# Attention with masked buckets: q and k turned by the host, softmax sums multiplied in at the end of a head pair

## The chip, the cores and the metric

The kernel runs on one core of a Trainium2 chip (trn2). The metric is device time in microseconds (us), from one launch. Of the core's engines the text uses TensorE (PE for matmuls, PEld for its weight loads), VectorE (DVE), ScalarE (ACT), GpSimd (POOL) and SyncE (SP, which here only issues DMAs).

## The reference

```
mask   = q_bucket[:, :, :, None] == k_bucket[:, :, None, :]   # bucket: signs of q @ proj, k @ proj (6 bits)
scores = where(mask, q @ k.T / sqrt(D), -1e9)
attn   = exp(scores - max);  attn /= sum(attn) + 1e-9
x      = (attn @ v) laid out as [B*S, H*D]                    # B 2, H 8, S 768, D 64
x      = moe(x):   4 experts, every token through all, weights p;  512 -> 1024 -> 512
out    = moe2(x):  8 experts, the best 2 of noisy logits per token; 512 -> 1024 -> 512
```

Only the attention and the seam to the first mixture of experts (MoE) are touched by the change.

## The kernel before, in words

**Attention.** There are 16 units (batch and head, `NU`), each of 6 tiles (`NI`) of 128 queries against 768 keys, so 96 tiles (`NG`). Values in float32 are kept as two parts, a high one in the PE's fp32r form and the rest, so that products are nearly exact.

For every unit the kernel loads q, k and v (`load`, L295) with tokens on the partitions, splits them (`split_q`, `split_k`, `split_q_rest`, `split_v`, all on POOL through the helpers at L273 and L276), and turns them on PE, since the scores need head dimensions on the partitions: `turn_half` makes three transposes of 128x128 for each half of k (L323) and three matmuls against the identity for each half of q's high part and of q's rest (L325), and ACT copies each half out of PSUM (L326). That is 18 PE instructions and 6 ACT copies a unit. Copies between the partition halves follow: `copy_q` and `lend_k` by DMA on SP (L283), `copy_k` on POOL (L285). `project_bits` (L356, 357) gives the hash bits, `mask_q` and `mask_k` (L360, L364) write them, scaled to 2^30, into the lower 64 rows of q2 and k2, so that the score matmul itself adds the mask.

For every tile: `scores` (four matmuls, L378, into a PSUM tile `big`), `clamp` (DVE, L385, takes the mask out and the row minimum), `exps` (ACT, L392, with the row sum into `rec`), `norm` (DVE adds 1e-9 at L398 and inverts at L400; POOL multiplies the whole 128x768 tile, L273), `turn` (six transposes on PE, L413; high part by ACT, L416; rest by DVE, L417), and for every three tiles `apply` (12 matmuls, L429 and L430, into `pa`). `gather` (ACT, L443) and `add_up` (DVE, L450) add the two halves of `pa` for a head into `xp`, and for every two heads `split` (POOL, L273; DVE, L458) writes the parts xth and xtl that the MoE reads.

**Order.** The attention is written out by hand in `tc.manual_schedule()`: every `block(order, lag, every, count, f)` puts calls of f into a list at a slot, counted in tiles, and a place within it; the sorted list is the order of the instructions on each engine. Nothing is bound to a time: an engine goes on as soon as its next instruction has its inputs.

**First MoE.** It follows as groups `n` of (batch, expert, quarter) with a hand-made order of their own; `first_layer` is L639 to L641, the second layer L657 to L659. Group 0 uses PSUM tiles `big`, group 1 needs the PSUM tiles that attention gives back. `stage_first` (L215) and `stage_part` (L169) load weights by SP into four buffers. Near the end of attention SP also issues `fill_scratch` (L155 to L163: zeros into the padding and the output, start values into the routing table) and ACT issues `small_inputs` (L136 to L139). The start of the kernel holds ten warming matmuls (L465), `projections` (L107), and the splitting of the first two w1 groups on DVE (`early_weights`, L178, L180).

Of the kernel before, what the change touches and what calls it, by code (L numbers as in the profile page):

```python
# [30 lines left out]
QB = 1  # L31
# [5 lines left out]
def lsh_attention_moe_kernel(ctx, tc, q, k, v, proj, probs, w1, w2, w_gate, w_noise, noise, w1b, w2b, out):  # L37
    nc = tc.nc
    B, H, S, D = q.shape
# [4 lines left out]
    NB = proj.shape[1]  # L44
# [26 lines left out]
    identr = const.tile([P, P], F32R, name="identr")  # L71
    nc.vector.tensor_copy(identr, ident)
# [27 lines left out]
    nc.vector.tensor_reduce(lessq[32:64], ident[32:64, 32:32 + NB], axis=AX.X, op=ALU.add, negate=True)  # L100
    lessk = const.tile([P, 1], F32, name="lessk")
    nc.vector.memset(lessk, 0.0)
    nc.vector.tensor_reduce(lessk[64:96], ident[64:96, 64:64 + NB], axis=AX.X, op=ALU.add, negate=True)


    def projections(pool):
        praw = pool.tile([P, NB], F32, name="praw", bufs=1)  # L107
        for r in range(2):
            nc.sync.dma_start(praw[r * D:(r + 1) * D], proj)
        ph = pool.tile([P, NB], F32R, name="ph", bufs=1)  # L110
        nc.vector.tensor_copy(ph, praw)
        pl = pool.tile([P, NB], F32R, name="pl", bufs=1)
        nc.vector.tensor_sub(pl, praw, v32(ph))
        pjq = pool.tile([P, P], F32R, name="pjq", bufs=1)
        pjk = pool.tile([P, P], F32R, name="pjk", bufs=1)
        pjl = pool.tile([P, P], F32R, name="pjl", bufs=1)
        for t in (pjq, pjk, pjl):
            nc.vector.memset(v32(t), 0.0)
        for o in (0, 32):
            nc.vector.tensor_scalar_mul(pjq[0:D, o:o + NB], v32(ph)[0:D], -1.0)  # L120
            nc.vector.tensor_scalar_mul(pjq[D:2 * D, o:o + NB], v32(pl)[D:2 * D], -1.0)
            nc.vector.tensor_copy(pjk[:, 64 + o:64 + o + NB], v32(ph))
            nc.vector.tensor_scalar_mul(pjl[0:D, o:o + NB], v32(ph)[0:D], -1.0)
            nc.vector.tensor_copy(pjl[D:2 * D, 64 + o:64 + o + NB], v32(pl)[D:2 * D])
        return pjq, pjk, pjl
# [9 lines left out]
    def small_inputs(n):  # L135
        nc.scalar.dma_start(pr.rearrange("p b i e -> p b (i e)"), probs.rearrange("(b p i) e -> p b (i e)", b=B, i=NI))  # L136
        nc.scalar.dma_start(nz.rearrange("p b i e -> p b (i e)"), noise.rearrange("(b p i) e -> p b (i e)", b=B, i=NI))
        nc.scalar.dma_start(wgn[:, :, 0:E2], w_gate.rearrange("(p c) e -> p c e", p=P))
        nc.scalar.dma_start(wgn[:, :, E2:], w_noise.rearrange("(p c) e -> p c e", p=P))  # L139
# [11 lines left out]
    yd = dram.tile([CAP, DM], F32, name="yd")  # L151
    table = dram.tile([E2 * ROWS_E, 2], I32, name="table")
    tv = table.rearrange("(e r) c -> e r c", e=E2)
    def fill_scratch(n):
        nc.sync.dma_start(x2d[0:PADS].rearrange("(t p) d -> p t d", p=P),  # L155
                          zero[:, :DM].unsqueeze(1).to_broadcast([P, PADS // P, DM]))
        nc.sync.dma_start(out.rearrange("(t p) d -> p t d", p=P),
                            zero[:, :DM].unsqueeze(1).to_broadcast([P, NT + PADS // P, DM]))
        nc.sync.dma_start(tv[1:, 0:CAP].rearrange("e (p s) c -> p e (s c)", p=SLOT_P),
                          pad_a.rearrange("p s c -> p (s c)").unsqueeze(1).to_broadcast([SLOT_P, E2 - 1, 2 * SLOT_S]))  # L160
        nc.sync.dma_start(tv[0, 0:CAP].rearrange("(h p s) c -> p h (s c)", h=2, p=SLOT_P),
                          pad_a.rearrange("p (h s) c -> p h (s c)", h=2))
        nc.sync.dma_start(tv[:, CAP:].rearrange("e (p j) c -> p e (j c)", p=P),  # L163
                            pad_b.rearrange("p j c -> p (j c)").unsqueeze(1).to_broadcast([P, E2, 2 * OVER_J]))
# [102 lines left out]
    with tc.tile_pool(name="at", bufs=2, side="right") as at, tc.tile_pool(name="psa", bufs=3, space=PSUM) as pss:  # L267
# [22 lines left out]
        def load(u):  # L290
            b, h = divmod(u, H)
            raws[u] = {}
            for nm, src, bufs in (("q", q, 2), ("k", k, 2), ("v", v, 3)):
                raws[u][nm] = ai.tile([P, NI, D], F32, tag=nm + "r", name=nm + "r", bufs=bufs)
                nc.sync.dma_start(raws[u][nm], src[b, h].rearrange("(p i) d -> p i d", i=NI))  # L295

        def split_q(u):
            qd = raws[u]["qd"] = ai.tile([P, NI, D], F32R, tag="qd", name="qd", bufs=QB)
            pool_scale(qd, raws[u]["q"], engine=nc.gpsimd)
# [28 lines left out]
        def turn_q(u, a):  # L328
            if a == 0:
                units[u] = {t: ai.tile([P, S], F32R, tag=t, name=t) for t in ("q1", "k1", "q2", "k2")}  # L330
# [981 lines left out]
```

## Time and profile before

| | |
|---|---|
| median of 3 runs | 1135.02 us (1134.3 to 1142.12) |
| the profiled execution's own time | 1136.44 us |
| its span, first to last instruction | 1134.7 us |
| PE, PEld busy | 97%, 88% of the span |
| DVE, ACT, POOL busy | 67%, 47%, 37% |
| mean granted TensorE clock | 0.987 of full speed |

A share is an average over stages. Attention fills about the first 272 us; the two MoE layers fill the rest. In rows of a timeline the first figure is the start in us from the span's start, the second the length; "[1.14 <-DMA q<-k]" says that the engine had been idle 1.14 us and what ended that. "x6" says that six neighbours are merged into a row.

### The profile page before, as it was taken

To read this page: it belongs to the slowest core of one execution; us is meant where nothing else is said; L and a number is where in the kernel's file an instruction comes from. 1 tells how busy PE (TensorE), PEld (TensorE's weight loads), DVE (VectorE), ACT (ScalarE), POOL (GpSimd) and SP (SyncE) were. 2 spreads that over 40 slices of the span, in tenths; PEclk is the share of its full clock that TensorE was granted. 3 is DMA by queue.
4 is the path that set the end of the run, shared out by engine and by line. 5 is a ranking of instruction groups with operands and counts; after the bars stand their busy time and mean duration, and the time that the engine had idled before them with its cause. 6 is when DMAs were issued, how large, how long until landed. Compare 5 with 4: busy or idle time off the path is not lost. (4 is left out here: it accounts for less than half of the span.)

```text
span 1134.7 us, 16731 instructions
## 1 busy us (share of the span) xinstructions
PE 1104.2 (97%) x6134; PEld 1003.4 (88%) x6135; DVE 756.1 (67%) x1549; ACT 529.2 (47%) x979; POOL 425.3 (37%) x464
## 2 busy tenths in 40 slices
PE   7999999998999999999999999999989999999997
PEld 5999999997888988899988988988879999999995
DVE  7999999996866565647766566535425666576651
ACT  4989999884334343333434342213214334443430
POOL 7888888861000000000000003025266626765434
PEclk8999999999999999999999999999799999999998
DMA  4222222182222122222322124114066468787864
GB/s 135 70 71 71 70 52 63 47 254 61 75 75 75 57 71 60 75 75 69 99 75 75 56 74 145 43 47 87 14 158 184 121 195 230 185 213 209 225 157 64
DMA packets 107166, 118.55 MB, mean 104 GB/s; under 512 B 13920, under 2 KB 78560, under 8 KB 106432
## 3 DMA queue, kind: packets, MB, share of 16 engines
q1 hardware_dynamic: 91948, 100.00, 30.2%
q0 software_dynamic: 9728, 15.18, 6.9%
q10 hardware_dynamic: 5404, 2.25, 0.9%
q8 instruction: 50, 0.82, 0.3%
q14 instruction: 36, 0.29, 0.1%
HBM read 90.60 MB, written 20.90 MB: 98 GB/s over the span
## 5 line engine op out<-in xcount | busy, mean ns | idle before, releaser
L178 POOL TENSOR_SCALAR w1h<-stage 128x1024 fp32r<-128x1024 f32 x4 | 5.1, 1277 | 418.5 <-PE sm L640 418.5
L1120 POOL DMA_INDIRECT xb<-x2d,at x96 | 104.1, 1085 | 35.2 <-issue 29.6
L273 POOL TENSOR_SCALAR ex<-ex,rec 128x768 f32<-128x768 f32 x96 | 92.4, 962 | 38.8 <-DVE rec L400 17.0
L417 DVE TENSOR_TENSOR el<-sm,eh 128x384 fp32r<-128x384 f32 x192 | 97.6, 548 | 12.9 <-ACT eh L416 11.4
L180 DVE TENSOR_TENSOR w2l<-stage,w2h 128x1024 fp32r<-128x1024 f32 x64 | 77.4, 1221 | 38.8 <-ACT w2h L176 36.1
L241 DVE SCALAR_TENSOR_TENSOR hl<-big,hh 128x864 fp32r<-128x864 f32 (+2 forms) x44 | 42.1, 957 | 88.6 <-ACT hh L239 68.5
L234 PE MATMUL big<-gh,w1h 128*128 128x432 f32 (+1 forms) x288 | 100.3, 348 | 0.6 <-ACT gh L945 0.6
L235 PE MATMUL big<-gl,w1h 128*128 128x432 f32 (+1 forms) x288 | 100.0, 347 | 0.1
L236 PE MATMUL big<-gh,w1l 128*128 128x432 f32 (+1 forms) x288 | 99.8, 346 | 0.0
L392 ACT ACTIVATE ex<-ms,mn 128x768 f32<-128x768 f32 x96 | 89.8, 935 | 7.9 <-DVE ms L385 3.7
L378 PE MATMUL big<-k,q 128*128 128x512 f32 (+1 forms) x384 | 90.6, 358 | 2.4 <-POOL k L364 2.4
L645 ACT ACTIVATE hh<-mx 128x384 fp32r<-128x384 f32 x72 | 37.8, 525 | 117.8 <-DVE mx L731 59.2
L385 DVE TENSOR_SCALAR_CACHE_REDUCE ms<-big 128x768 f32<-128x768 f32 x96 | 90.4, 942 | 3.2 <-PE big L378 2.9
L239 ACT ACTIVATE hh<-big 128x864 fp32r<-128x864 f32 (+2 forms) x44 | 35.7, 811 | 118.5 <-PE big L236 85.7
L659 PE MATMUL big<-w2h,hl 128*128 128x512 f32 x224 | 88.4, 395 | 0.5 <-DVE hl L646 0.5
L416 ACT CAST eh<-sm 128x384 fp32r<-128x384 f32 x192 | 82.0, 479 | 14.3 <-PE sm L413 13.3
L657 PE MATMUL big<-w2h,hh 128*128 128x512 f32 x224 | 88.2, 394 | 0.0
L658 PE MATMUL big<-w2l,hh 128*128 128x512 f32 x224 | 88.1, 393 | 0.0
L180 DVE TENSOR_TENSOR w1l<-stage,w1h 128x1024 fp32r<-128x1024 f32 x64 | 79.2, 1238 | 12.9 <-ACT w1h L176 10.6
L963 POOL DMA_INDIRECT out_dram<-xg,lts x28 | 52.9, 1889 | 76.6 <-DVE xg L961 66.8
L413 PE MATMUL sm<-ident,ex 128*128 128x128 f32 x576 | 80.5, 274 | 1.1 <-POOL ex L273 0.9
L413 PEld LDWEIGHTS sm<-ident,ex 128*128 128x128 f32 x576 | 65.9, 140 | 5.3 <-POOL ex L273 1.5
(277 smaller groups left out, 3142.1 us busy)
## 6 DMA issues: line engine op xcount, KB each, us to landing
stage<-in_moe_w_dram SPq DMA_DIRECT2D x96, 512.0 KB
stage<-in_moe_w_dram SPq DMA_DIRECT2D x58, 256.0 KB
yd<-yt SPq DMA_DIRECT2D x24, 216.0 KB
ya<-yd SPq DMA_DIRECT2D x6, 864.0 KB
out_dram<-zero SPq DMA_DIRECT2D x1, 4096.0 KB
qr<-in_q_dram SPq DMA_DIRECT2D x16, 192.0 KB
kr<-in_k_dram SPq DMA_DIRECT2D x16, 192.0 KB
vr<-in_v_dram SPq DMA_DIRECT2D x16, 192.0 KB
```

The source lines that it names most:

```text
L180: rest.tensor_sub(lo, st, v32(hi))
L234: nc.tensor.matmul(o, wh[:, d, fs], xh[:, d, cols], start=(d == 0), stop=False)
L235: nc.tensor.matmul(o, wh[:, d, fs], xl[:, d, cols], start=False, stop=False)
L236: nc.tensor.matmul(o, wl[:, d, fs], xh[:, d, cols], start=False, stop=(d == ND - 1))
L273: engine.tensor_scalar(o, i, scale, bias, op0=ALU.mult, op1=ALU.add)
L378: nc.tensor.matmul(ps[:, n0:n1], w_[:, qs], x_[:, n0:n1], start=st, stop=not st)
L385: nc.vector.tensor_scalar(ms, ps[:, :S], MASKED, 3.0e38, op0=ALU.min, op1=ALU.min, accum_out=mn)
L392: nc.scalar.activation(ex, ms, AF.Exp, bias=mn, scale=-1.0, accum_out=rec)
L413: nc.tensor.transpose(pt[:, c * P:(c + 1) * P], ex[:, cc * P:(cc + 1) * P], ident)
L417: nc.vector.tensor_sub(el[:, cs, js], ptv, v32(eh)[:, cs, js])
L659: yield lambda: nc.tensor.matmul(outs[j], hl[:, k, js], wh[:, i], start=False, stop=sp)
L1120: nc.gpsimd.indirect_dma_start(out=xb[:, b], out_offset=None, in_=x2d.rearrange("t (g x) -> (t g) x", g=4), in_offset=bass.IndirectOffsetO ...
```

## The change

The host (outside the timed launch) hands q and k over as one array `qk` with the head dimension on the rows: rows 0 to 63 hold q of a head and rows 64 to 127 its k, in 768 columns; and `proj` already laid out in a 128x128 tile.

- `load` reads one 128x768 tile z a unit; `scale_z`, `split_z`, `split_z_rest` (POOL, 128x768 each) scale and split q and k together. The first unit does it on DVE in halves (`open_z`, `open_z_rest`).
- `spread_k` (three copies) and `spread_q` (one) bring parts to the other 64 partitions, by SP's DMAs of 64x768; for the first unit on ACT and POOL. All of `turn_half` and its callers go.
- `project_bits` keeps three matmuls a half.
- `norm` goes. `exps` writes its row sums into a column of a tile `rec` of 128x32 per unit; `invert` (DVE, three instructions a unit) adds 1e-9, inverts and turns it in blocks of 32; `note` (four DMAs on SP) writes rows of it to DRAM (`norms`), `spread_norms` (one DMA) reads them back as 64 equal rows into `share`.
- `gather` has two ACT copies a half (into xa and xb), `add_up` and the new `share_out` (a multiplication with `share`) run on POOL once for two heads, 128x768 each. The last pair has its own `finish`, on POOL, DVE and ACT, in parts.
- `early_weights` becomes `early_stage` and eight `early_split` on POOL, later in the order. `small_inputs` is issued by SP. `fill_scratch` is cut into six pieces, which SP issues in MoE groups 1 to 6, behind that group's weight loads.
- All slots of the order are new; each is now one number, in tiles.

```diff
 def load(u):
-    for nm, src, bufs in (("q", q, 2), ("k", k, 2), ("v", v, 3)):
-        raws[u][nm] = ai.tile([P, NI, D], F32, tag=nm + "r", ...)
-        nc.sync.dma_start(raws[u][nm], src[b, h].rearrange("(p i) d -> p i d", i=NI))
+    z = ai.tile([P, S], F32, tag="z", name="z", bufs=2)
+    if u == 0:
+        for a, queue in enumerate((nc.sync, nc.scalar)):
+            queue.dma_start(z[:, a * QW:(a + 1) * QW], qk[b, h][:, a * QW:(a + 1) * QW])
+    else:
+        nc.sync.dma_start(z, qk[b, h])
...
+def scale_z(u):
+    pool_scale(z, z, halve)
+def split_z(u):
+    pool_scale(parts_for(u)["q1"], raws[u]["z"])
+def split_z_rest(u):
+    split_rest(units[u]["q2"], raws[u]["z"], units[u]["q1"])
+def moved(u, o, i, engine=nc.scalar):
+    if u > 0:
+        nc.sync.dma_start(v32(o), v32(i))
...
+def spread_k(u, part):
+    o, i = ((k1[0:D], q1[D:2 * D]), (k2[0:D], q1[D:2 * D]), (k1[D:2 * D], q2[D:2 * D]))[part]
+    moved(u, o, i, nc.gpsimd if part == 1 else nc.scalar)
+def spread_q(u):
+    moved(u, q1[D:2 * D], q1[0:D])
...
-def turn_half(a, src, dst, rows, scale):
...
 def exps(g):
-    nc.scalar.activation(ex, ms, AF.Exp, bias=mn, scale=-1.0, accum_out=rec)
+    nc.scalar.activation(ex, ms, AF.Exp, bias=mn, scale=-1.0, accum_out=recs[u % 2][:, i:i + 1])
-def norm(g, part):
-    if part == 0:
-        nc.vector.tensor_scalar_add(rec, rec, 1e-9)
-    else:
-        nc.vector.reciprocal(rec, rec)
-        pool_scale(ex, ex, rec)
+def invert(u):
+    nc.vector.tensor_scalar_add(rec[:, :NI], rec[:, :NI], 1e-9)
+    nc.vector.reciprocal(rec[:, :NI], rec[:, :NI])
+    nc.vector.transpose(rates[u], rec)
+def note(u):
+    for g in range(4):
+        nc.sync.dma_start(norms[u].rearrange("(i g r) -> g i r", g=4, r=32)[g], rec[32 * g:32 * g + NI])
+def spread_norms(u):
+    nc.sync.dma_start(shares[u // 2][mine], norms[u:u + 1].to_broadcast([D, S]))
...
-def gather(hf):
-    nc.scalar.copy(xp[mine, qs], pa[rest, :QW])
-def add_up(hf):
-    nc.vector.tensor_add(x, x, o)
+def gather(hf, part):
+    nc.scalar.copy(pairs[u // 2][part][mine, qs], pa[(rest, mine)[part], :QW])
+def add_up(pair):
+    nc.gpsimd.tensor_add(xa, xa, xb)
+def share_out(pair):
+    nc.gpsimd.tensor_mul(xa, xa, shares.pop(pair))
...
+block(-12.56, NI, NU, load, begin=(-43.40, -14.36,))
+block(-7.82, NI, NU, scale_z, first=1)
+block(-5.52, NI, NU, split_z, first=1)
+block(-5.03, NI, NU, split_z_rest, first=1)
+block(-5.02, NI, NU, load_v, begin=(-22.88, -12.53,))
+block(-4.74, NI, NU, spread_k, 0, begin=(-11.98,))
+block(-4.51, NI, NU, project_bits, 0, begin=(-15.79,))
+block(-2.85, NI, NU, spread_k, 2, begin=(-18.14,))
+block(-2.80, NI, NU, spread_k, 1, begin=(-14.56,))
+block(-2.52, NI, NU, project_bits, 1, begin=(-8.36,))
+block(-1.40, NI, NU, spread_q, begin=(-4.53,))
+block(-1.34, NI, NU, mask_q, begin=(-4.45,))
+block(-0.89, NI, NU, mask_k, begin=(-2.15,))
+block(-0.20, 1, NG, scores, begin=(-0.76,))
+block(6.48, NI, NU, invert)
+block(10.49, NI, NU, note)
+block(11.73, NI, NU, spread_norms)
+block(0.00, 1, 2, early_stage, begin=(14.31, 21.80,))
+block(22.45, 2 * NI, NU // 2 - 1, add_up)
+block(23.36, 2 * NI, NU // 2 - 1, share_out)
...
+            fill_scratch(n - 1)
```

## Rows read from the trace of the kernel before

**Rows 1.** Stretches: busy us of PE, PEld, DVE, ACT, POOL; granted clock; DMA share; GB/s.
```profile
16.00:22.00 6.00, 4.86 (x19) 4.38 (x20) 3.05 (x9) 2.81 (x6) 5.35 (x7) 0.50 0.33 100
...
120.00:150.00 30.00, 30.00 (x215) 27.98 (x215) 28.67 (x81) 27.64 (x65) 26.23 (x31) 1.00 0.25 67
```

**Rows 2.** Timeline of DVE: clamps of tiles 1, 7, 91 and 96.
```profile
16.16 0.94 DVE L385 TENSOR_SCALAR_CACHE_REDUCE ms<-big 128x768 f32<-128x768 f32 x1
...
29.16 0.94 DVE L385 TENSOR_SCALAR_CACHE_REDUCE ms<-big 128x768 f32<-128x768 f32 x1
...
242.66 0.96 DVE L385 TENSOR_SCALAR_CACHE_REDUCE ms<-big 128x768 f32<-128x768 f32 x1
...
252.90 0.93 DVE L385 TENSOR_SCALAR_CACHE_REDUCE ms<-big 128x768 f32<-128x768 f32 x1
```

**Rows 3.** Timeline of PE: half of q's rest, half of k, each with its successor.
```profile
107.52 0.35 PE L325 MATMUL sm<-identr,qrest 128*64 128x128 f32 x3
107.71 0.84 PE L413 MATMUL sm<-ident,ex 128*128 128x128 f32 x6
...
121.18 0.49 PE L323 MATMUL sm<-ident,kd 128*128 128x128 f32 x3
121.43 0.94 PE L378 MATMUL big<-k,q 128*128 128x512 f32 x4
```

**Rows 4.** Groups of PEld by line, 120.98 to 151.28 (two units).
```profile
L323 PEld LDWEIGHTS sm<-ident,kd 128*128 128x128 f32 x12 | 1.5, 141 | 0.1
...
L325 PEld LDWEIGHTS sm<-identr,qd 128*64 128x64 f32 x12 | 1.2, 136 | 0.2 <-DVE el L417 0.2
```

**Rows 5.** Timeline of DVE: the last small step of a tile, and an add_up.
```profile
118.05 0.15 DVE L400 RECIPROCAL rec<-rec 128x1 f32<-128x1 f32 x1
118.12 0.94 DVE L385 TENSOR_SCALAR_CACHE_REDUCE ms<-big 128x768 f32<-128x768 f32 x1
...
104.87 0.53 DVE L450 TENSOR_TENSOR xp<-xp,pa 64x384 f32<-64x384 f32 x1
```

**Rows 6.** A transposition on DVE, from the answer on tile yt.
```profile
L1143 DVE STREAM_TRANSPOSE yt<-padded x24: 698/705/715, 884.7 to 1086.1; 128x512 f32<-128x512 f32 x24
```

**Rows 7.** Groups of ACT by line: q's copies out of PSUM.
```profile
L326 ACT ACTIVATE q<-sm 64x384 fp32r<-64x384 f32 x64 | 30.5, 481 | 13.7 <-PE sm L325 11.2
```

**Rows 8.** Groups of POOL by line: the multiplication of norm, a subtraction.
```profile
L273 POOL TENSOR_SCALAR ex<-ex,rec 128x768 f32<-128x768 f32 x96 | 92.4, 962 | 38.8 <-DVE rec L400 17.0 <-PE sm L413 11.8 <-ACT ex L392 7.1
...
L276 POOL TENSOR_TENSOR qrest<-qr,qd 128x384 fp32r<-128x384 f32 x16 | 17.0, 1063 | 0.2
```

**Rows 9.** Timeline of SP: copies across partitions, one alone, one ahead of loads.
```profile
72.04 0.47 SPq L283 DMA_DIRECT2D q<-q  x1
75.93 0.47 SPq L283 DMA_DIRECT2D q<-k  x1
```

**Rows 10.** A stretch after the first of them: clock, DMA share, GB/s.
```profile
74.00:75.00 1.00, 1.00 0.05 12
```

**Rows 11.** Timeline of PE: the matmul that waits for the second of them.
```profile
80.31 0.44 PE L356 MATMUL sm<-q,pjl 128*128 128x384 f32 x1 [1.14 <-DMA q<-k]
```

**Rows 12.** Timeline of the start: POOL, then PEld.
```profile
4.80 0.51 POOL L273 TENSOR_SCALAR qd<-qr 128x384 fp32r<-128x384 f32 x1 [2.52 <-DMA qr<-in_q_dram]
...
15.21 0.30 PEld L378 LDWEIGHTS big<-k,q 128*128 128x128 f32 x2 [2.77 <-POOL k L364]
```

**Rows 13.** Timeline of the seam to the MoE: ACT, then PE.
```profile
260.36 0.94 ACT L392 ACTIVATE ex<-ms,mn 128x768 f32<-128x768 f32 x1 [3.01 <-DMA nz<-in_moe_noise_dram]
...
272.09 0.45 PE L639 MATMUL sm<-xth,w1h 128*128 128x384 f32 x1 [1.15 <-DVE xp L450]
```

**Rows 14.** Timeline of SP: the costliest piece of fill_scratch to issue.
```profile
232.80 9.40 SPq L159 DMA_DIRECT2D table<-pad_a  x1
```

**Rows 15.** Waits of SP, 330 to 460: us in total, times, longest.
```profile
SPq L215 <- DVE w2l L180: 82.6, 8, 10.5
SPq L169 <- DVE mw L621: 37.0, 9, 5.0
```

More of the change, by code (lines that the diff above doesn't have):

```diff
@@ L430, in apply @@
                 nc.tensor.matmul(pa[:, :QW], vx[:, c], el[:, c], start=False, stop=(c == NI - 1))
-        def gather(hf):
+        def gather(hf, part):
             u, half = divmod(hf, 2)
             b, h = divmod(u, H)
-            del halves[hf]
-            pa = sums.pop(hf)
-            if hf % 4 == 0:
-                pairs[u // 2] = at.tile([P, S], F32, tag="xp", name="xp")
-            xp = pairs[u // 2]
+            pa = sums[hf]
+            if hf % 4 == 0 and part == 0:
+                pairs[u // 2] = [tl.tile([P, S], F32, tag=t, name=t, bufs=XB) for t in ("xa", "xb")]
             mine = slice((h % 2) * D, (h % 2 + 1) * D)
@@ L454, in split, with finish @@
             cs = slice(b * S, (b + 1) * S)
+            xa, _ = pairs[pair]
             if part == 0:
-                pool_scale(xth[:, c, cs], pairs[pair], engine=nc.gpsimd)
+                pool_scale(xth[:, c, cs], xa, engine=nc.gpsimd)
             else:
-                nc.vector.tensor_sub(xtl[:, c, cs], pairs.pop(pair), v32(xth)[:, c, cs])
+                nc.vector.tensor_sub(xtl[:, c, cs], xa, v32(xth)[:, c, cs])
+                del pairs[pair]
+        def finish(n):
+            pair = NU // 2 - 1
+            b, c = divmod(pair, H // 2)
+            xa, xb = pairs[pair]
+            what, step = divmod(n, 3)
+            rows = slice(0, D) if what == 0 else slice(D, 2 * D)
+            cols = slice(0, S) if what == 0 else slice((what - 1) * QW, what * QW)
+            x, hi, lo = (t[rows] for t in (xa, xth[:, c, b * S:(b + 1) * S], xtl[:, c, b * S:(b + 1) * S]))
+            if step == 0:
+                engine = nc.vector if what == 2 else nc.gpsimd
+                more = sums.pop(4 * pair + 3)[rows, :QW] if what == 2 else xb[rows, cols]
+                engine.tensor_add(x[:, cols], x[:, cols], more)
+                engine.tensor_mul(x[:, cols], x[:, cols], shares[pair][rows, cols])
+            elif step == 1:
+                if what == 2:
+                    nc.scalar.copy(hi[:, cols], x[:, cols])
+                else:
+                    pool_scale(hi[:, cols], x[:, cols])
+            else:
+                nc.vector.tensor_sub(lo[:, cols], x[:, cols], v32(hi)[:, cols])
         NU = B * H
@@ L466, in lsh_attention_moe_kernel, with block, early_stage, early_split @@
             events = []
-            def block(order, lag, every, count, f, *args, begin=()):
-                for n in range(count):
-                    slot = begin[n] if n < len(begin) else (lag + n * every, order)
-                    events.append((*slot, f, n, args))
+            def block(at, every, count, f, *args, begin=(), first=0):
+                for n in range(first, count):
+                    events.append((begin[n - first] if n - first < len(begin) else at + n * every, f, n, args))
             early_w1 = []
-            def early_weights(n):
+            def early_stage(n):
                 stage_first(n)
-                plain[n] = split_plain(n, nc.vector)
+                plain[n] = [wa.tile([P, ND, 2, P], F32R, tag=t, name=t, bufs=2) for t in ("w1h", "w1l")]
+            def early_split(k):
+                n, part = divmod(k, 4)
+                ds = slice(part % 2 * (ND // 2), (part % 2 + 1) * (ND // 2))
+                hi, lo = plain[n]
+                if part < 2:
+                    pool_scale(hi[:, ds], raw1[n][:, ds])
+                else:
+                    split_rest(lo[:, ds], raw1[n][:, ds], hi[:, ds])
             def stage_weights(n):
```

261 lines of the change are left out of this document (124 added, 137 removed).

## The prediction

> **What bounds the kernel now.** I read four views in this order. First the busy shares: PE is busy for 97% of the span at a granted clock of 0.987, all other engines for two thirds or less, so time is won where PE has less to do or waits less. Second the table of stretches [rows 1]: in attention the other engines are nearly full too. Of 30 us PE has 30.00, DVE 28.67, ACT 27.64, POOL 26.23, and the reader is to see that a saving on PE alone is worth something only as far as DVE, ACT and POOL also shrink. Third the starts of the clamps, one a tile [rows 2]: tile 7 (first of unit 1) at 29.16, tile 91 (first of unit 15) at 242.66, so a unit takes (242.66 - 29.16) / 14 = 15.25 us; ahead of it lies a start of 16.16 us to the first clamp, behind it a seam from the last clamp at 252.90 to the first MoE matmul that needs attention's PSUM. Fourth single instructions in the timelines, for prices. Everything after the seam is PE-bound MoE that the change leaves as it is, except for what SP issues there.
>
> So the sum has three terms: 15 units' worth of steady work (14 periods, and the 13.0 us of unit 0, in which the turning for units 1 and 2 is done), the start, and the seam.
>
> **PE in a unit.** It loses 18 instructions. Ends of matmuls are modelled, so I price by the distance to the next start [rows 3]: half of q, three matmuls, 107.71 - 107.52 = 0.19; half of k, three transposes, 121.43 - 121.18 = 0.25. A unit has four halves of q (high part and rest) and two of k: 4 x 0.19 + 2 x 0.25 = 1.26 us. Nothing is added on PE, since the hash keeps six matmuls. PE's unit becomes 15.25 - 1.26 = 13.99 us, and 15 x 1.26 = 18.9 us is the first term.
>
> A rule of the Trainium skill (Perfetto Trace Analysis, Identifying the Most-Contended Engine) says that the matmuls' busy share is a poor measure of how full PE is, and that the weight loads' share is a good one. By this rule PE had room left in attention, since its weight loads fill 27.98 of 30 us [rows 1], and the removed ones, three groups of twelve in two units [rows 4], would count by their own length. What that would make of the time is the first rival below.
>
> **DVE in a unit.** It loses twelve small steps of norm, each 0.07 by the distance to the next start (118.12 - 118.05) and 0.15 by its length, and two add_ups of 0.53 [rows 5]: 0.84 to 1.8, and 1.06. It gains invert: two small steps of the same kind (0.07 to 0.15) and a transposition of 128x32. The only transposition in the trace has 512 columns and takes 0.70 [rows 6]; a small step's 0.07 is the lower end. So 0.2 to 1.0 is added, and the net is -0.9 to -2.7; I take -1.6, with invert near its lower end, since 32 columns are nearer to a small step than to 512. DVE's 28.67 of 30 is 14.6 a unit; it becomes 13.0, and 13.7 at worst. Both lie under PE's 13.99, so DVE hides, with 0.3 us to spare at worst; without that cover its excess would come on top of each unit.
>
> **ACT and POOL in a unit.** ACT loses six copies out of PSUM of 0.48 [rows 7] and gains two of the same shape for gather: -1.9, from 14.1 to 12.1. POOL loses six multiplications of 0.96 [rows 8] and two subtractions of 1.06 (q's and k's rests), 7.9, besides the other splits of q and k and one copy. It gains scale_z and split_z (same shape as the multiplication, 0.96 each), a rest of twice the columns (2 x 1.06), and for two units one add_up and one share_out of twice the columns, 2.12 each, so 2.12 a unit: 6.2. At most 13.3 - 1.7 = 11.6, hidden. The early w1 splits, now on POOL too, are a few us once, in the middle of units with over 2 us to spare each.
>
> **SP in a unit.** This is where the change adds waits. SP had five DMAs a unit (three loads, two copies) and gets eleven (two loads, four copies, four notes, one read back); at 0.47 to issue [rows 9] that is 5.2 of 14 us. How long a copy takes to land is bounded by two rows: the one issued alone at 72.04 has moved its data by about 74, since in the next microsecond the DMA share is 0.05 [rows 9, 10], so 2.0 us is the lower end; the one issued at 75.93 ahead of loads lets PE go at 80.31 [rows 11], 4.4 us. I take 2.0 to 4.4 for every kind of new DMA, for the write to DRAM and the read back as well, which the trace doesn't show at this size.
>
> The tight one is spread_q: it overwrites the lower half of q1, which the hash matmuls and two copies read, so it can be issued only after project_bits' second half (slot -2.52) and has to land before the unit's first scores (-0.20). That is 2.32 tiles of 13.99 / 6 us, 5.4 us, against 0.47 + 2.0 to 4.4. It fits, with 0.5 us left at the bad end. Ahead of it on SP stand note's four DMAs (4 x 0.47 = 1.9 us). Their input, invert, is four tiles older than their slot, so SP will have issued them while it waited for project_bits; I cost them at nothing. If they fall into the window after all, a unit is late by up to 1.9 + 0.47 + 4.4 - 5.4 = 1.4 us. What queues behind spread_q is spread_norms, which waits for note's landing, and then the next unit's copies, for which most of a unit is left.
>
> **The start.** Now the first full scores wait for mask_k at 15.21, after POOL began on q at 4.80 [rows 12]; the first clamp is at 16.16. After: z's halves are the first DMAs of two queues, so work can begin near 4.8 or earlier. Four opening steps on DVE at about 0.53 (2.1), three matmuls (0.5, an estimate from 0.19 for three smaller ones), two bits (1.1), mask_k on POOL (0.96), scores (0.94 [rows 3]): 4.8 + 5.6 = 10.4, and the first clamp near 10.7, since the second half of z and proj come by a queue that starts later. ACT's copies for the other halves (three of 64x768, 0.96 each by twice [rows 7]) lie beside that. The gain is 5.5; the ends are 2 and 6.5, since now the clock falls to 0.50 from 16 to 22 us after PE had little to do [rows 1], and the same may come earlier.
>
> **The seam.** From 252.90 to 272.09 it takes 19.2 us [rows 2, 13]. ACT stands 3.01 us behind the issue of small_inputs, which goes to SP, and PE 1.15 us for the last add_up. New on the path: the last unit's sums have to travel through DRAM before DVE's part of finish frees `pa`. From the last clamp: clamp and exps 1.9, invert 0.2 to 1.0, note 1.9 to issue and 2.0 to 4.4 to land, the read back 2.0 to 4.4, add and multiply 1.1: 9.1 to 14.7 us, under the 19.2 - 4.2 = 15.0 us that PE has to do there anyway. So the gain is 3.0 + 1.2 = 4.2; ends +2 (DVE stands in that wait while the MoE's splits queue behind it) and -6.
>
> **fill_scratch in the MoE.** The start values of the table take 9.40 us to issue [rows 14], the second piece no more, so up to 18.8 us in one group. SP idles 82.6 / 8 + 37.0 / 9 = 14.4 us a group [rows 15]. At worst a weight load is 4.4 us late, and it is for the group after the next: nothing.
>
> **Sum.** -18.9 - 5.5 - 4.2 = -28.6 us. Against the profiled execution's own 1136.4 that is 1107.8; the median of the runs is 1.4 lower, which gives 1106.4. The case's own range is 1100 to 1113.
>
> **Rivals.**
> 1. The weight loads are the measure of PE's time (the rule above). The removed ones are 1.5 for k, 1.2 for one part of q and, its twin taken as equal, 1.2 for the other [rows 4], 3.9 in two units, so 1.95 a unit; at the share of now, 27.98 of 30, that is 2.1 us of time a unit and 31.4 in all: 1136.4 - 31.4 - 5.5 - 4.2 - 1.4 = 1094. For it: DVE, ACT and POOL all shrink by more than 1.3. Against: DVE at 13.0 leaves 15.25 - 2.1 = 13.15 barely reachable.
> 2. spread_q lands late and PE waits before each unit: 0.6 us costs 9 (1115), 1.4 costs 21 (1127). For it: PE already waited 1.14 us for such a copy. Against: the slots leave 5.4 us.
> 3. SP becomes the bound, and the kernel is slower. If everything on SP is serial, a unit is note 1.9 + 4.4, three copies 1.4 + 4.4, spread_q 0.47 + 4.4: 17.0 us, +1.75 a unit, 26 in all, and 1135 + 26 - 9.7 = 1151. It decides from a unit of 15.25 + 9.7 / 15 = 15.9 us. Against: with 2.0 to land the same chain is 9.8 us, and the three copies don't wait for note.
>
> **How the numbers follow.** Forecast 0.62, rival 1 0.14, rival 2 0.19, rival 3 0.05. The range 1095 to 1121 takes in the forecast, most of rival 1 and the better half of rival 2. A measurement tells about 1%, 11 us. Over 1% faster is below 1123.7: the forecast, rival 1 and three quarters of rival 2, 0.90; within 1% the rest of rival 2 and a little of rival 3, 0.06; slower 0.04.
>
> **What would show it.** Right: clamps of successive units 13.5 to 14.2 us apart; first clamp at 10 to 12; from the last clamp to the first MoE matmul on `sm` 14 to 17 us; PE still without gaps in attention, ACT and DVE below 93% there; the rest from that matmul to the end as long as now, 1134.7 - 272.1 = 862.6. Wrong: PE waits for a DMA of q1 at each unit's first scores (rival 2); SP never idle and units over 15 us apart (rival 3); units at 13.2 or less (rival 1); or a MoE longer than 862.6 by over 3 us, with waits for stage loads near group 7.

## The result, and the profile after

The changed kernel takes 1106.99 us (median of 4 runs, 1105.27 to 1122.99) against 1134.66 us of the kernel before on the same chip (4 runs, 1131.45 to 1142.12). The ratio is 0.9732 with a 95% interval of 0.9671 to 0.9792: faster, by 2.7%; they leave out the run of 1122.99 us, which ran in a slower state of the chip (mean granted clock 0.980, against 0.989 in the other three). The profiled execution has an own time of 1105.56 us and a span of 1103.5 us, at a mean granted clock of 0.989. Forecast were 1106.4 us and a range of 1095 to 1121.

The marks of the stages first: the clamps of tiles 1, 3, 7, 91 and 96 on DVE in the changed kernel (start, duration, instruction, and in brackets what it idled for), which answer to [rows 2].

```profile
10.48 0.96 DVE L387 TENSOR_SCALAR_CACHE_REDUCE ms<-big 128x768 f32<-128x768 f32 x1 [1.49 <-PE big L380]
...
15.76 0.96 DVE L387 TENSOR_SCALAR_CACHE_REDUCE ms<-big 128x768 f32<-128x768 f32 x1 [0.81 <-PE big L380]
...
23.49 0.95 DVE L387 TENSOR_SCALAR_CACHE_REDUCE ms<-big 128x768 f32<-128x768 f32 x1
...
216.76 0.95 DVE L387 TENSOR_SCALAR_CACHE_REDUCE ms<-big 128x768 f32<-128x768 f32 x1
...
228.13 0.95 DVE L387 TENSOR_SCALAR_CACHE_REDUCE ms<-big 128x768 f32<-128x768 f32 x1
```

And on PE the two waits between tiles 2 and 3, and the first MoE matmul on `sm`, which answers to the last line of [rows 13].

```profile
11.76 0.69 PE L358 MATMUL sm<-q,pjh 128*128 128x384 f32 x1 [0.27 <-POOL q L273]
...
13.66 0.69 PE L358 MATMUL sm<-q,pjh 128*128 128x384 f32 x1 [0.90 <-POOL q L276]
...
243.38 0.44 PE L695 MATMUL sm<-xth,w1h 128*128 128x384 f32 x1 [1.15 <-DVE xa L496]
```

From these marks the whole difference of the spans, 31.2 us, can be laid out:

| stage | before, us | after, us | difference | forecast |
|---|---|---|---|---|
| to the first clamp | 16.16 | 10.48 | -5.68 | -5.5 |
| tiles 1 to 7 (unit 0) | 13.00 | 13.01 | 0.0 | -1.3 |
| 14 units, tiles 7 to 91 | 213.50 | 193.27 | -20.2 | -17.6 |
| tiles 91 to 96 | 10.24 | 11.37 | +1.1 | 0 |
| last clamp to first matmul on `sm` (the seam) | 19.19 | 15.25 | -3.9 | -4.2 |
| from there to the end | 862.6 | 860.1 | -2.5 | 0 |

A unit is now 193.27 / 14 = 13.805 us instead of 15.25. The 14 units in one stretch each, the kernel before and the changed one (columns as in [rows 1]):

```profile
29.16:242.66 213.50, 211.66 (x1511) 198.25 (x1509) 202.28 (x568) 195.25 (x448) 182.32 (x215) 1.00 0.28 78
```

```profile
23.49:216.76 193.27, 192.79 (x1269) 177.29 (x1266) 180.68 (x413) 174.69 (x393) 132.89 (x124) 1.00 0.46 117
```

So PE's busy time fell by (211.66 - 192.79) / 14 = 1.35 us a unit and its idle time, 1.84 and 0.48 us in all, by 0.10. The stage of tiles 1 to 7, which gained nothing, in both:

```profile
16.16:29.16 13.00, 11.73 (x64) 10.06 (x65) 9.72 (x31) 9.10 (x21) 11.11 (x15) 0.75 0.16 47
```

```profile
10.48:23.49 13.01, 11.59 (x55) 9.23 (x54) 9.91 (x22) 8.69 (x18) 7.97 (x9) 0.74 0.37 91
```

Two more stretches of the changed kernel; the second line answers to the 30 us shown there:

```profile
10.00:24.00 14.00, 12.58 (x62) 10.15 (x63) 10.42 (x22) 8.96 (x19) 8.92 (x10) 0.76 0.36 89
...
120.00:150.00 30.00, 29.93 (x198) 27.63 (x197) 28.36 (x68) 27.41 (x63) 21.05 (x19) 1.00 0.48 123
```

PE is full in the steady state as before, and per unit it is DVE 28.36 x 13.805 / 30 = 13.05 us, ACT 12.6, POOL 9.7. The waits of SP from 20 to 215 us (total, times, longest):

```profile
SPq L418 <- POOL xa L473: 24.6, 6, 4.7
SPq L326 <- PE sm L358: 22.8, 9, 3.6
```

SP stands in waits of this kind for a good part of attention, so it is not full, and in the same stretch the only wait recorded for PE is 0.2 us, once, for DVE: none is for the DMA of q1. What is new at the end of a unit, the inversion on DVE and the way of the sums through DRAM, in the last unit: DVE, then SP, then POOL.

```profile
233.34 0.16 DVE L404 TENSOR_SCALAR rec<-rec 128x6 f32<-128x6 f32 x1
233.53 0.19 DVE L405 RECIPROCAL rec<-rec 128x6 f32<-128x6 f32 x1
233.76 0.21 DVE L407 STREAM_TRANSPOSE rect<-rec 128x32 f32<-128x32 f32 x1
...
234.00 1.31 SPq L412 DMA_DIRECT2D norms<-rect  x4
236.50 0.48 SPq L418 DMA_DIRECT2D share<-norms  x1
...
239.78 1.27 POOL L497 TENSOR_TENSOR xa<-xa,share 64x384 f32<-64x384 f32 x1 [1.84 <-DMA share<-norms]
```

The inversion takes 233.89 - 233.34 = 0.55 us to the next start; from the first DMA to the first use of what comes back are 5.8 us. The first MoE matmul on `sm` does not wait for this: it is let go by DVE's addition at 242.76, which waited for ACT's copy of `pa`, and ACT for PE.

### The profile page after: what moved, and what is told of

It is laid out like the page before. It is cut to its first block, busy times and chain, and to the rows that moved or that the text cites. A ratio compares the mean times of both kernels' runs of the same rounds, so it can differ in the third digit from the quotient of the medians.

```text
span 1103.5 us, 15809 instructions
## 1 busy us (share of the span) xinstructions
PE 1081.4 (98%) x5846; PEld 977.4 (89%) x5847; DVE 728.6 (66%) x1364; ACT 508.4 (46%) x918; POOL 368.8 (33%) x364
## 3 DMA queue, kind: packets, MB, share of 16 engines
q10 hardware_dynamic: 4092, 2.41, 0.9%
## 5 line engine op out<-in xcount | busy, mean ns | idle before, releaser
L436 DVE TENSOR_TENSOR el<-sm,eh 128x384 fp32r<-128x384 f32 x192 | 102.7, 549 | 16.7 <-ACT eh L435 15.1
L435 ACT CAST eh<-sm 128x384 fp32r<-128x384 f32 x192 | 86.8, 478 | 17.6 <-PE sm L432 16.9
L432 PE MATMUL sm<-ident,ex 128*128 128x128 f32 x576 | 91.1, 275 | 1.0 <-DVE el L436 0.6
L179 DVE TENSOR_TENSOR w1l<-stage,w1h 128x1024 fp32r<-128x1024 f32 x62 | 75.7, 1221 | 14.4 <-ACT w1h L175 9.4
L432 PEld LDWEIGHTS sm<-ident,ex 128*128 128x128 f32 x576 | 70.8, 141 | 11.7 <-DVE el L436 4.9
L1195 PE MATMUL sm<-hh,w2h 128*128 128x432 f32 x192 | 68.5, 357 | 0.6 <-issue 0.6
```

Source lines behind the costliest of these rows:

```text
L179: rest.tensor_sub(lo, st, v32(hi))
L432: nc.tensor.transpose(pt[:, c * P:(c + 1) * P], ex[:, cc * P:(cc + 1) * P], ident)
L436: nc.vector.tensor_sub(el[:, cs, js], ptv, v32(eh)[:, cs, js])
```

## The experiments

My theory: in the steady state PE sets the unit and the 18 instructions that left it are the gain, provided DVE shrinks with it; start and seam come as the prediction's parts say. Rivals: DVE or POOL set the unit before; start and seam came from something else. The kernel before took 1124.94 us (median) on one of the chips used and 1150.92 us (one run) on another, so stages are compared by the marks of each kernel's own profile.

**PE's instructions back.** The changed kernel with 18 small matmuls and transposes a unit that nobody reads.

```
+def turn_again(k):   # parts 0 to 3: like half of q; 4, 5: like half of k
...
+    for i in range(HALF):
+        if part < 4: nc.tensor.matmul(t[:D, i * P:(i + 1) * P], pjs[0][:, 0:D], pjs[0], start=True, stop=True)
+        else: nc.tensor.transpose(t[:, i * P:(i + 1) * P], ident, ident)
...
+block(0.50, 0.97, NU * NI, turn_again)
```

> The changed kernel with 18 PE instructions a unit put back that nothing reads: twelve matmuls of 64 columns of weights against 128 columns and six 128x128 transposes, in six groups of three, one a tile. Nothing else differs. Theory (PE's order of instructions sets the unit): a unit takes 13.81 + 1.26 = 15.07 us, 14.9 to 15.2, and the span grows by 16 x 1.26 = 20 to about 1124. Rival (another engine sets the unit and PE's work was hidden): the unit stays under 14.3 and the span under 1111.

Measured: clamp of tile 7 at 22.20, of tile 91 at 238.21, so 15.43 us a unit; ratio 0.9955 (0.9939 to 0.9972). The stretch of this kernel, and the added lines in it:

```profile
120.00:150.00 30.00, 30.00 (x220) 28.26 (x218) 26.69 (x60) 25.23 (x58) 18.55 (x18) 1.00 0.40 106
...
L511 PE MATMUL sm<-pjh 128*64 128x128 f32 x27 | 3.1, 224 | 0.0
L513 PE MATMUL sm<-ident 128*128 128x128 f32 x12 | 2.0, 272 | 0.0
```

PE is gapless, DVE has fallen to 26.7 of 30. The theory holds; the price is 15.43 - 13.81 = 1.62 us for 18 instructions at these slots rather than 1.26. Why it is more than the distances to the next start, which I had read off one neighbour, was not taken apart.

**DVE's steps back.** PE stays relieved; DVE alone gets twelve small steps and two additions a unit on tiles of their own.

```
...
+def tiny(g):
+    nc.vector.tensor_scalar_add(dum[0][:, :1], dum[0][:, :1], 1e-9)
+    nc.vector.reciprocal(dum[0][:, :1], dum[0][:, :1])
+def more_add(hf):
+    nc.vector.tensor_add(dum[1][:D], dum[1][:D], dum[1][:D])
...
+block(1.39, 1, NG, tiny)
+block(7.70, HALF, 2 * NU, more_add)
```

> Tests whether the load that left VectorE counted. VectorE alone gets back per tile the two small steps (0.07 to 0.15 us each) and per half of a unit one 64x384 addition (0.53 us), on tiles of their own that nobody reads; TensorE, ScalarE, GpSimd and the copies stay as in the changed kernel. Theory (TensorE sets the unit and VectorE has 13.05 us of the 13.81): VectorE comes to 13.05 + 6 x 0.14 + 2 x 0.53, that is 14.9 us, or 15.9 if each of the small steps takes its full row; it takes over and the unit comes out at 14.9 to 16.0, so without the move of the additions and the reciprocals TensorE's saving would have been worth little. Rival (VectorE's room inside the unit takes it up): unit at or under 14.2.

Measured: tile 7 at 22.57, tile 91 at 237.91, so 15.38 us a unit; one run took 1120.44 us. Its 14 units in one stretch, and one pair of the small steps with its successor on DVE:

```profile
22.57:237.91 215.34, 205.73 (x1265) 174.82 (x1263) 211.49 (x609) 176.90 (x394) 139.54 (x124) 1.00 0.41 105
```

```profile
137.35 0.13 DVE L519 TENSOR_SCALAR dum<-dum 128x1 f32<-128x1 f32 x1
137.51 0.16 DVE L520 RECIPROCAL dum<-dum 128x1 f32<-128x1 f32 x1
137.59 0.54 DVE L436 TENSOR_TENSOR el<-sm,eh 128x384 fp32r<-128x384 f32 x1
```

Now DVE is the full one. A dependent pair takes 0.16 + 0.08 = 0.24 us by the starts, six pairs 1.4, two additions 0.9: 13.05 + 2.3 = 15.4, the unit. So PE's relief hangs on DVE's. The two halves are not alike, though. With PE's work back the unit is 15.43, and before it was 15.25: DVE's relief alone would have bought nothing. The other run puts back more than had left: DVE is busy 211.49 / 14 = 15.11 us a unit here and was 202.28 / 14 = 14.45 in the kernel before, because the inversion stays and the added steps stand beside it. DVE is full here at 211.49 of 215.34 us, a share of 0.982; with the load of the kernel before it would set the unit at 14.45 / 0.982 = 14.7 us (an estimate from these rows). So by this estimate PE's relief alone would have bought some 0.5 of the 1.45 us. In the kernel before, PE was the full engine (1.84 us idle in the 14 units) and DVE stood close behind it.

**The multiplication back.** Per tile again: rec added to and inverted on DVE, ex multiplied on POOL ahead of the transposes; no DMA of sums. In the second kernel the additions of the halves also go back to DVE.

```
...
+def norm(g, part):
+    if part == 0: nc.vector.tensor_scalar_add(rec, rec, 1e-9)
+    else:
+        nc.vector.reciprocal(rec, rec)
+        pool_scale(ex, ex, rec)
...
-block(6.48, NI, NU, invert)
+block(1.35, 1, NG, norm, 0)
+block(1.45, 1, NG, norm, 1)
...
-block(2.78, 1, NG, turn, 0)
+block(3.78, 1, NG, turn, 0)
```

> The changed kernel with norm as before: DVE's two small steps and POOL's multiplication for every tile, turn and all behind it one tile later, no invert, note, spread_norms, share_out. PE has the changed kernel's work. Theory (PE sets the unit, DVE lies just under it at 13.1): DVE gains twelve small steps of 0.07 to 0.15 and loses invert (about 0.5), so 13.4 to 14.4, and the unit takes 13.8 to 14.4 us; span 1103 to 1112. Rival (taking norm out of the tiles is what paid): unit above 14.6, span above 1114.

> As the one before, and add_up on DVE as before too (one ACT copy a half, DVE adds out of PSUM; the last pair splits like the others). So only the turning of q and k is left of the change in attention. Theory (the unit goes to the fullest of PE and DVE): DVE 14.4 to 15.2 a unit, so it takes over from PE: unit 14.4 to 15.1 us, span 1113 to 1123, which gives back a third to all of the 1.45 us a unit. Rival (PE alone counts): unit 13.8 to 14.0 and span at most 1106.

Measured: 20.35 and 19.75 us a unit, spans 1187.5 and 1183.4 us; the second has a ratio of 1.0517 (1.0495 to 1.0538). Both are misses. The waits of PE in the first of them, 40 to 220 us, and its stretch:

```profile
PE big L380 <- POOL k L366: 22.0, 9, 3.7
PE sm L358 <- POOL q L276: 11.3, 9, 1.3
```

```profile
120.00:150.00 30.00, 20.04 (x125) 17.02 (x123) 20.89 (x60) 18.66 (x41) 21.83 (x22) 1.00 0.18 47
```

No engine is full. POOL has 21.83 x 20.35 / 30 = 14.8 us of work a unit, which I had left out of the sum, and works in order: each multiplication waits for its tile's inverted sum, and behind it stand the split of the next unit's z and the masks, for which PE waits. The slots are mine, so the 20 us are a price of this order, not of the multiplication. What the runs show is that in this order the multiplication and the splits of q and k do not go together in POOL's queue; what taking the multiplication out is worth by itself stays open.

**Where the seam came from, first try.** The copies of the small inputs back on ACT.

```
-def small_inputs(n):  nc.sync.dma_start(...)
+def small_inputs(n):  nc.scalar.dma_start(...)
```

> The changed kernel with the four small loads before the MoE issued by ACT again, at the same slot. The prediction's account of the seam (ACT stood 3.0 us behind them, and PE with it): from the last clamp to the first MoE matmul on sm 15.25 + 3.0 = 18 us, span about 1106.5. Rival (the seam is full of PE work that has to be done anyway, and ACT's stand is covered): 15.2 to 16 us, span 1103 to 1104.

Measured: last clamp 226.40, first matmul on `sm` 241.65: 15.25 us, to the hundredth that of the changed kernel, although ACT stands behind the issues again, 2.41 us for the 3.01 of [rows 13]:

```profile
229.59 0.48 ACT L435 CAST eh<-sm 128x384 fp32r<-128x384 f32 x1 [2.41 <-DMA stage<-in_moe_w_dram]
```

In the changed order this stand costs nothing. For the kernel before the run doesn't settle it, because there the last tile's exps, which came at 260.36 behind that stand, were followed by norm: DVE's reciprocal at 263.98, then POOL's multiplication (its row names PE's transposes, which ended last before it), for which PE waited.

```profile
264.32 1.44 POOL L273 TENSOR_SCALAR ex<-ex,rec 128x768 f32<-128x768 f32 x1 [5.79 <-PE sm L413]
...
265.82 0.87 PE L413 MATMUL sm<-ident,ex 128*128 128x128 f32 x6 [0.86 <-POOL ex L273]
```

At most these 0.86 us can be the stand's price on PE there, which is read off the rows and not tested.

**Second try: the lag of the transposes.** Only slots change.

```
-block(2.78, 1, NG, turn, 0)
-block(3.33, 1, NG, turn, 1)
-block(6.27, HALF, 2 * NU, apply, 0)
+block(3.26, 1, NG, turn, 0)
+block(4.35, 1, NG, turn, 1)
+block(6.88, HALF, 2 * NU, apply, 0)
...
-block(7.38, HALF, 2 * NU, apply, 2)
-block(7.46, HALF, 2 * NU, gather, 0)
+block(8.46, HALF, 2 * NU, apply, 2)
+block(8.53, HALF, 2 * NU, gather, 0)
...
```

> Where the seam's 3.9 us come from, after the copies of the small inputs have been ruled out. In the kernel before the multiplication by the inverted sums stood between a tile's exps and its transposes, so the transposes were listed about 3.2 and 4.3 tiles behind the clamp and the last of a half's matmuls on pa 8.4; the changed kernel lists them at 2.78, 3.33 and 7.38. This kernel moves only these slots (turn, apply, gather) back by 0.5 to 1.1 tiles. Theory (the seam is the work that TensorE still has to do for the last tiles when the last clamp is done, and this lag sets it): unit unchanged at 13.7 to 13.9, from the last clamp to the first MoE matmul on sm 16.8 to 19 us instead of 15.25, span longer by 1.5 to 3.5. Rival (the lag only trades against the time from tile 91 to 96, or the seam is bound by the chain from the last exps through pa): from tile 91 to that matmul at most 0.7 us more than 26.62, whatever the seam alone shows.

Measured: last clamp 233.67, first matmul on `sm` 252.68, a seam of 19.01 us; from tile 91 at 222.26 to that matmul 30.42 instead of 26.62. What PE had to do in the seam, as a stretch and by groups of its lines: the kernel before, the changed one, and this one.

```profile
252.90:272.09 19.19, 16.31 (x101) 15.24 (x100) 10.33 (x28) 7.22 (x17) 3.34 (x4) 1.00 0.33 82
...
L429 PE MATMUL pa<-eh,vx 128*128 128x384 f32 x14 | 5.1, 361 | 0.9 <-DVE xp L450 0.9
...
L413 PE MATMUL sm<-ident,ex 128*128 128x128 f32 x27 | 4.1, 274 | 0.9 <-POOL ex L273 0.9
```

```profile
228.13:243.38 15.25, 14.10 (x88) 13.58 (x87) 9.15 (x18) 7.36 (x16) 7.87 (x7) 1.00 0.49 149
...
L448 PE MATMUL pa<-eh,vx 128*128 128x384 f32 x12 | 4.2, 352 | 0.0
...
L432 PE MATMUL sm<-ident,ex 128*128 128x128 f32 x18 | 2.9, 272 | 0.0
```

```profile
233.67:252.68 19.01, 16.42 (x103) 15.60 (x101) 11.53 (x20) 9.53 (x21) 9.01 (x7) 1.00 0.45 134
...
L448 PE MATMUL pa<-eh,vx 128*128 128x384 f32 x14 | 5.1, 364 | 0.7 <-ACT xb L465 0.7
...
L432 PE MATMUL sm<-ident,ex 128*128 128x128 f32 x26 | 4.3, 272 | 0.0
```

With the old lag 26 transposes and 28 matmuls on `pa` (half of them from eh, as shown, half from el) are left when the last clamp is done, nearly the 27 and 28 of the kernel before; with the new one 18 and 24. PE's busy time in the seam is 16.31 us before, 14.10 after and 16.42 here: 2.2 of the 3.9 us are work that PE, following a tile more closely now that the multiplication no longer stands between exps and transposes, has done ahead of the last clamp. The other 1.7 us are PE's waits, 2.88 us before and 1.15 after; the 0.9 us each for POOL and DVE in the groups before are gone. So the lag gives the seam back, as expected. The other part of what was expected failed: the unit grew too, to (222.26 - 21.22) / 14 = 14.36 us, with PE's weight loads for the transposes waiting 11.2 us for DVE's `el` in 40 to 215 us. How much of the unit's gain hangs on the closer lag stays open; I did not try it together with PE's instructions.

**The start.** The first two w1 groups are staged and split on DVE before the first clamp again, as in the kernel before.

```
-block(0.00, 1, 2, early_stage, begin=(14.31, 21.80,))
+block(0.00, 1, 2, early_stage, begin=(-14.30, -14.20,))
-block(0.00, 1, 8, early_split, begin=(19.53, 21.30, 22.30, 26.59, 26.65, 31.23, 32.30, 33.30,))
...
+block(0.00, 1, 4, early_halves, begin=(-4.40, -4.30, -0.60, -0.50,))   # both steps on DVE
```

> The changed kernel with the first two w1 groups loaded right behind the first q, k and v and split on DVE in unit 0, as before the change. The prediction put the start's gain down to q and k coming turned. By that, the first clamp stays at 10.5 to 11.5 us and tile 7 comes 0 to 2 us later for DVE's splits (2 x 1.9 us). Rival (the start was slow for the weights in the queues and on DVE): first clamp at 13 or later, tile 7 over 26 instead of 23.5.

Measured: first clamp at 15.98, of tile 7 at 26.56. DVE in this kernel, then in the kernel before:

```profile
12.00 1.31 DVE L273 TENSOR_SCALAR w1h<-stage 128x1024 fp32r<-128x1024 f32 x1
13.35 2.71 DVE L276 TENSOR_TENSOR w1l<-stage,w1h 128x1024 fp32r<-128x1024 f32 x1
15.98 0.94 DVE L387 TENSOR_SCALAR_CACHE_REDUCE ms<-big 128x768 f32<-128x768 f32 x1
```

```profile
13.79 0.68 DVE L178 TENSOR_SCALAR w1h<-stage 128x1024 fp32r<-128x1024 f32 x1
14.51 1.73 DVE L180 TENSOR_TENSOR w1l<-stage,w1h 128x1024 fp32r<-128x1024 f32 x1
```

With q and k still coming turned, 15.98 of the 16.16 us are back. The rival is right in that the first clamp stood behind four splits of w1 on DVE: the turn alone would have been worth 0.2 us. But the splits were not all that held it in the kernel before. There the first full scores stood behind POOL's mask_k [rows 12]:

```profile
12.88 2.28 POOL L364 TENSOR_SCALAR k<-bits,lessk 64x768 fp32r<-64x768 f32 x1
...
15.21 0.62 PE L378 MATMUL big<-k,q 128*128 128x512 f32 x2 [2.45 <-POOL k L364]
```

The scores end at 15.21 + 0.62 = 15.83, the splits at about 16.2. So both had to go, and moving the splits alone would have gained some 0.3 us as these rows stand. How much more it would have gained by a faster mask_k (2.28 us beside the splits, 1.33 in the changed kernel) is open: no run has the splits moved and q and k as before.

**fill_scratch back in attention.** All six pieces run ahead of the MoE, at slot 99.8, instead of one by one inside it.

> The changed kernel with all of fill_scratch issued at the end of attention again (slot 99.8, ahead of the last unit's note), and nothing of it in the MoE groups. Theory (SP is in order and stood 15 us behind the table's start values there): note and the read back of the last unit come 15 us late, PE waits for the last pair, and the seam grows from 15.25 to 22 to 26 us, span 1110 to 1115. Rival (the place of fill_scratch doesn't matter): seam and span as in the changed kernel within 1.5 us.

Measured: seam 15.25 as in the changed kernel, but a span of 1113.5 us, 10.4 more than the kernel with the small inputs on ACT, on the same chip, one run each. The longest wait of PE from 215 to 330, and SP:

```profile
PE big L714 <- ACT w2h L175: 8.0, 1, 8.0
```

```profile
225.28 7.06 SPq L156 DMA_DIRECT2D out_dram<-zero  x4
232.38 2.60 SPq L158 DMA_DIRECT2D table<-pad_a  x1
235.03 5.14 SPq L160 DMA_DIRECT2D table<-pad_a  x1
...
```

Size right, place wrong: not the last pair but the weights of the MoE's first group came late behind 16 us of issues. So the piecewise fill inside the MoE is worth about 10 us beside the fill at this place, and shows no cost where it now stands: the rest after the seam is no longer than in the kernel before.

**spread_q twice.** Each copy of q1's lower half is issued two times.

> The changed kernel with spread_q's DMA issued twice in units 1 to 15, the second behind the landing of the first. It measures how much room the copy has before the unit's first scores. By the prediction's lower end (2.0 to land, 5.4 us of room) the second lands at 2 x 2.5 = 5.0 and nothing changes: unit 13.8. By its upper end (4.4 to land) the second is 4.3 us late, and the unit grows to about 18 us, span 1165. In between, PE's wait for it tells the room.

Measured: 14.56 us a unit. The wait of PE from 40 to 220, and SP's two issues:

```profile
PE big L381 <- DMA q<-q: 6.5, 11, 0.7
```

```profile
134.43 3.00 SPq L326 DMA_DIRECT2D q<-q  x2
```

The second issue, 0.47 us long, comes only when the first has landed: 3.00 - 0.47 = 2.5 us from one issue to the next, an upper end for the landing. A copy that comes some 2.5 us later makes PE wait 0.6 us, so the single one has about 1.9 us to spare.

**The order of the start.** Unit 1's mask projections behind the scores of tiles 2 and 3; then four unread matmuls ahead of the first scores; then both.

```
-block(-4.51, NI, NU, project_bits, 0, begin=(-15.79,))
+block(-4.51, NI, NU, project_bits, 0, begin=(-15.79, 2.85,))
-block(-2.52, NI, NU, project_bits, 1, begin=(-8.36,))
+block(-2.52, NI, NU, project_bits, 1, begin=(-8.36, 3.85,))
...
+def keep_warm(n):
+    nc.tensor.matmul(warm[:, 512:1024], ones, zero.bitcast(BF16)[:, :512], start=True, stop=True)
...
+block(-8.30, 0.01, 4, keep_warm)
```

> The order at the start alone: the mask projections of unit 1 move behind the scores of tiles 2 and 3, so that TensorE, in order, does not stand before tile 2's scores for GpSimd's split of unit 1's z (0.27 and 0.90 us of waits). Theory (those waits and the 2.4 us of projections at half clock hold tile 2 and 3): the third clamp, 15.76 us in the changed kernel, comes 1.5 to 3 us earlier, and tile 7 (23.49) 1 to 3 earlier. Rival (the first tiles are bound by the half clock or by VectorE's splits whatever the order, or unit 1 then becomes late by as much): tile 7 within 0.5 us of 23.49.

> The clock at the start alone: four bf16 matmuls that nobody reads (512 columns) stand between the mask projections of unit 0 and the first scores. In the changed kernel the granted clock is 0.50 from about 10.8 to 17.2 us, after a stretch in which TensorE did little. Theory (the fall comes from that idle stretch): the half clock goes or gets shorter, and tile 7 (23.49) comes 1 to 2 us earlier. Rival (the four matmuls, some 1.7 us at half clock, do not reach, or delay the first scores): first clamp and tile 7 the same or up to 1 us later.

> The version that is to beat both: the mask projections of unit 1 behind the scores of tiles 2 and 3, and four unread matmuls ahead of the first scores. Theory (the reordering is worth some 1.2 to 2 us by tile 7, 21.37 against 21.75 to 23.49 elsewhere; the unread matmuls cost nothing and keep the clock at full): third clamp near 13, tile 7 at 20.5 to 21.4, clock 1.00 between 10 and 24 us, ratio to the kernel before 0.970 to 0.975, which the interval of the changed kernel (0.967 to 0.979) does not tell from it. Rival (unit 1 was what the first tiles waited for in the end): tile 7 not before 21.7.

Measured: third clamp 13.14 and tile 7 at 21.37 in the first; 14.50 and 21.95 in the second; 12.57 and 20.71 with both. In the first the clock was at its lower level for a part of the 14 us of the lines below (0.88), in the other two not. The second alone settles nothing: its stretch, and that of the kernel with the fill in attention, whose start is the changed kernel's, have the same clock and the latter has tile 7 at 21.75.

```profile
10.00:24.00 14.00, 11.99 (x72) 9.65 (x71) 11.65 (x26) 10.33 (x22) 10.04 (x11) 1.00 0.44 113
```

```profile
10.00:24.00 14.00, 11.99 (x73) 9.68 (x72) 11.81 (x27) 10.54 (x23) 10.04 (x11) 1.00 0.45 113
```

So the level of 1.2 GHz that the changed kernel's profile shows there (0.76 is a mixture of 0.50 and 1.00) does not come in every execution, and where it comes tile 7 is 23.49 - 21.75 = 1.7 us later. It does not follow the idle time ahead of the first scores either: PE had waited 1.53 us for ACT there in the changed kernel, and 2.18 us in the one with the small inputs on ACT, and the clock fell in both; it had waited 2.19 us in the kernel with the fill in attention, and there it stayed. The reordering is worth 21.75 - 20.71 = 1.0 us with the full clock. Both together, in 5 runs: 1096.18 us against 1124.94, ratio 0.9739 (0.9715 to 0.9764). That does not tell it from the changed kernel's 0.9732 (0.9671 to 0.9792); it beats the kernel before, and whether it beats the changed one is not shown.

## Why the prediction was right, point by point

**The unit** was right in its mechanism and somewhat small: -1.445 us for -1.26. The term that was mis-sized is PE's 18 instructions, which I priced by one start-to-start distance each: PE's busy time fell by 1.35 us a unit, and put back at other slots they cost 1.62. The other 0.10 us are PE's idle time, chiefly its waits for the copies between q and k [rows 11], 1.8 us in two waits between 60 and 210 us, which are gone.

**Unit 0** was to gain as much as the others, -1.3, and gained nothing. The lower clock is not the reason, because the kernel before has it in this stage too (0.75 and 0.74). PE's busy time there is nearly the same, 11.73 and 11.59 us: the 15 turning instructions of the kernel before (2.4 us in their groups) are gone, and with the closer lag four matmuls on `pa` (1.5 us) and two more transposes have come into it. At the full clock the same start took 11.48 us for tiles 1 to 7 in the kernel with the fill in attention; the kernel before has no profile at that clock.

**DVE** was costed to the tenth: 14.6 to 13.0, measured 13.05. That PE's saving counts only as far as DVE shrinks was said, and the run with DVE's steps back bears it out: the unit is 15.38 and the gain of PE is gone, with 0.66 us a unit more on DVE than it had before. The sign that DVE would stay under 93% failed narrowly, 28.36 of 30 us being 94.5%, since the unit came out shorter than forecast.

**ACT and POOL** hide, as was said: ACT came to 12.6 us, 0.5 more than the 12.1 forecast, POOL to 9.7, under its bound of 11.6.

**The start** came out at -5.68 for -5.5, for half the reason. The step that failed is "now the first full scores wait for mask_k at 15.21", taken as the only thing that holds the first clamp. It is a true row, but DVE's four w1 splits held the clamp to 16.16 as well. Without the move of early_split, which the prediction costed only as a few us on POOL, the gain would have been 0.2 us.

**The seam** came out at -3.9 for -4.2, mostly for another reason. The step that failed is "ACT stands 3.01 us behind the issue of small_inputs", priced in full: in the changed order such a stand of 2.41 us costs nothing, and in the kernel before at most 0.86 us of it reached PE. The 1.15 us on DVE's last addition are there before and after. The gain is 2.2 us of work, by the closer lag, and 1.7 us of waits. It is not all won: 1.1 us are given back between tiles 91 and 96, where PE is now busy 10.97 us instead of 9.99, and unit 0 has taken up some of the same work. The bound on the DRAM round trip (9.1 to 14.7 us, hidden) was right: 239.78 - 228.13 = 11.65 us to its first use.

**The DMAs on SP**: spread_q fits, with more room than the 0.5 us at the bad end; the landing is at or under 2.5 us, so the second rival's 4.4 was an end that did not come. The third rival fell by SP's idle time.

**Weight loads as the measure.** Of the 30 us weight loads fill 27.63, for 27.98 before: 0.92 and 0.93. So a unit went down nearly in proportion to them: their time in it from 14.22 us to 12.71, a factor of 0.89, the unit by a factor of 0.91. That agrees with the rule of the Trainium skill (Perfetto Trace Analysis, Identifying the Most-Contended Engine), which judges PE by the share of its weight loads. What was off in that rival is its 1.95 us, the sum of the busy times of the removed groups: the busy time of all weight loads fell by 1.50 us a unit over the 14 units. Groups overlap; from 120.98 to 151.28 [rows 4] those of the kernel before add up to 31.1 us, and the engine is busy for 28.28.

**After the seam** 2.5 us went that I had at nothing. PE's busy time there is the same in both, 844.59 and 844.53 us with 4348 matmuls, so it is idle time. Whether the move of fill_scratch made it was not separated, and it lies within the spread of executions: in the experiments whose instructions behind the seam are the changed kernel's, this rest took 849.0 to 881.2 us.

In all, the sum was 28.6 us and the spans differ by 31.2. Of the three terms the first rests on the reason that was given, the start on half of it, and the seam on little of it; that these two came out so near is luck, and so is that the forecast of 1106.4 us lies within 0.6 us of the median, since the interval of the ratio alone is some 14 us wide.

## What to carry to other kernels

Where two engines are both above nine tenths in a stretch, put the load of each back alone before crediting either, and no more of it than had left: here PE's load by itself brings back the whole unit, and DVE's does so with 0.66 us a unit on top. Before a stall at the start or at a seam is credited to one wait, list every engine's work that ends at that moment: two of my three terms had a true row, a right size and a cause that was half of it or less. And a step per tile on an engine that works in order can tie everything else in its queue to the tile's pace, although the engine is not full: POOL was busy for 21.83 of 30 us.

## What was not expected of the hardware

A start value's issue on SP took 9.40 us before [rows 14] and in the MoE of the changed kernel takes 0.44:

```profile
319.43 0.44 SPq L158 DMA_DIRECT2D table<-pad_a  x1
```

In the kernel with the fill in attention the same piece takes 2.60 and the next 5.14, right behind four issues of zeros that take 7.06. So the piece itself is not long to issue; in these runs it was so behind the zeros. With spread_q twice, the second copy was held on SP until the first had landed, some 2.5 us, although both are issued from the same queue. And the lower clock after the start came in some executions of nearly the same instructions and not in others (0.76 and 1.00 over the same 14 us).
